# A fused attention, token-mix and channel kernel: divisions and low words moved to GpSimd, new planner costs and tables, own banks for the last products

## The chip, the cores and the metric

The kernel runs on one core of a Trainium2 chip. The metric is the device time of the program in microseconds (us); smaller is better. The engines are named as in the profile: PE (TensorE's matmuls), DVE (VectorE), ACT (ScalarE), POOL (GpSimd) and SP (the queue that issues the transfers).

## What is computed

Four batches of 576 tokens, eight heads of 64. Three layers follow each other:

```python
# 1. attention, window 32; heads 4..7 take every 4th token of a window of 128
scores = scale * q @ k.T, masked;  attn = softmax(scores)
x = attn @ v                                   # (4, 576, 512)
# 2. token mix
xk = mu_k * x + (1 - mu_k) * x_prev            # x_prev: the token before
xr = mu_r * x + (1 - mu_r) * x_prev
v = relu(xk @ w_k) ** 2 @ w_v                  # 512 -> 1024 -> 512
y = sigmoid(xr @ w_r) * v
# 3. low rank over tokens, then a channel MLP, 512 -> 2048 -> 512
u = y + (y.T @ U @ V).T
out = u + relu(u @ w_ch1) @ w_ch2
```

## The kernel before

*Attention* goes by units of a batch, a part of its tokens and a pair of heads. `attend` does one unit (the four of the first part of batch 0), `attend2` two at once. A unit has stages: scores on PE ("qk"), minimum and mask on DVE (`low`, L549), exponentials on ACT (L558), the inverse of the sums on DVE (`inv`, L563 and L564), the division (`norm`, L575, on the engine that the table `NORM_ENG` names for the unit), transposes on PE ("tr", L655 and L741), a copy to SBUF on ACT, the product with v ("pv", L667 and L759), and a copy into the x of the batch. A *visit* is one step of a pair of units: the later half of the old pair (tr, pv) and the scores of the new.

*Token mix.* The 2304 tokens go in 8 chunks of 288. `mix` makes one operand of one pair of heads: the difference `d` = x - x_prev on POOL (L359), then d * mu + x_prev on DVE (L796). For chunk 0 that is multiplied with the whole fp32 weights (`r_row` L855 with four products for each pair, `k_row` L870, then L839). For later chunks operand and weight are split into a high and a low fp32r word and each product is three (high x high, L842; low weight, L843; low operand, L844). The high word is a copy on ACT, the low word a subtraction on the engine that `XK_ENG` names for chunk 1, and on POOL for later chunks. Weights arrive as 64-bit floats in 20 pieces and are converted by `cv_bits`: one ACT step, two DVE steps with a scalar (L398, L399) and two with two tensors (L401, L404).

*Stage 3.* `product` multiplies blocks of 256 by seven products in place of eight (L1076 to L1078), in groups of 256 and four times 512 tokens; `ch1` sums them (L1113) and makes the hidden block as `hh` (ACT) and `hl` (DVE, L1091 and L1133); `ch2` multiplies these with the rows of the second weight into four banks (L1155 to L1157) and, at the last block of a group, adds u and stores (L1175). In the last group the output o = 3 is split at column 384 (`ENDS`), so its ends are stored separately.

*What sets the order.* Every operation is first recorded, with its engine, an estimated duration (`pe`, `dve`, `act`, `sub`, `normed`), what it reads and writes. The code order of the recording comes from the tables at the top: `MIX0` and `MIX` (after which quantum of a chunk which operand of the next is mixed), `VISIT0` and `VISIT` (at which quanta attention takes a step), `LOADS`, `UV_AT`, `PREP`, `SPLIT` (when which weight piece is split). `plan` then runs a list schedule over the estimates, 24 times, with ranks from a pass backwards, from which `EARLIER` takes microseconds for some kinds; DVE and POOL exclude each other in it for operations marked `lock`. The best pass is issued as one order for each engine. Into gaps of PE of more than 0.6 us in the plan it puts matmuls on `zero` (fillers, L1358), whose results are not used. So all engines run fixed orders, and an operation that waits holds up all behind it on its engine.

## Time and profile before

| | us |
|---|---|
| median of 3 runs | 745.29 (744.68 to 746.07) |
| profiled execution, its own time | 745.44 |
| its span, first to last instruction | 743.7 |
| PE busy | 734.8 (99%) |
| DVE busy | 564.2 (76%) |
| ACT busy | 393.9 (53%) |
| POOL busy | 365.2 (49%) |
| chain that ended last | PE 89%, DVE 7%, ACT 2%, issue 1% |

[...] The chain is followed back from the last instruction, at each step to what released it. PE's granted clock was 9 tenths or more in all 40 slices of the span. Times in timelines are from the start of the span, and matmuls overlap, so their pace is the distance of their starts.

### The profile page before, as it was taken

The page shows a single profiled execution, that of the slowest core. Times are in us where ns is not written, and L with a number is a line of the kernel's source. Part 1 is how long each engine was busy: PE and PEld are TensorE (multiplying, and loading weights), DVE is VectorE, ACT ScalarE, POOL GpSimd, SP SyncE. Part 2 cuts the span into 40 slices and gives each one's busy share as a digit, 9 for nine tenths or more (in the row PEclk, how much of TensorE's full clock was granted, in tenths as well). Part 3 has the DMA queues.
Part 4 walks back from the last instruction along what each step waited for, and adds up shares of the span by engine and source line. Part 5 has one row for each costly group of instructions (what it writes and reads, how often), then busy time and mean ns, then how long its engine had stood idle before and what let it go on. Part 6 is the DMA issues. An engine that isn't in the chain of part 4 may idle for free.

```text
span 743.7 us, 18335 instructions
## 1 busy us (share of the span) xinstructions
PE 734.8 (99%) x6936; PEld 678.0 (91%) x6936; DVE 564.2 (76%) x1353; ACT 393.9 (53%) x1003; POOL 365.2 (49%) x380
## 2 busy tenths in 40 slices
PE   8999999999999999999999999999999999999998
PEld 6777999999999999999999989889889988898886
DVE  6999999899998945885679687676988765575532
ACT  5696795858585746473546444444444433343310
POOL 0100274746473635283776477344878544365500
PEclk9999999999999999999999999999999999999999
DMA  8877338658757640557633451134413212141001
GB/s 317 290 260 238 124 114 274 229 198 264 229 167 252 210 129 15 204 174 244 220 104 114 142 185 43 53 133 139 152 43 109 91 43 86 43 138 62 15 1 57
DMA packets 53224, 109.78 MB, mean 148 GB/s; under 512 B 5648, under 2 KB 15888, under 8 KB 53136
## 3 DMA queue, kind: packets, MB, share of 16 engines
q1 hardware_dynamic: 53136, 108.62, 44.0%
q8 instruction: 54, 0.88, 0.5%
q14 instruction: 34, 0.28, 0.1%
HBM read 86.05 MB, written 22.54 MB: 146 GB/s over the span
## 4 chain that ended last, share of the span: by engine, by line
PE 89%; DVE 7%; ACT 2%; issue 1%; DMA 0%; POOL 0%; DVEq 0%
PE psM L842 10%; PE psM L843 10%; PE psM L844 10%; PE psS L1157 9%; PE psS L1155 9%; PE psS L1156 9%; PE psM L1076 8%; PE psM L1078 8%; PE psM L1077 8%; PE psS L759 2%; DVE wx L401 1%; PE psS L703 1%; DVE wx L398 1%; PE psM L839 1%; DVE wx L404 1%
## 5 line engine op out<-in xcount | busy, mean ns | idle before, releaser
L359 POOL TENSOR_TENSOR cl<-sums,ch 128x512 fp32r<-128x512 f32 x72 | 98.3, 1366 | 83.1 <-ACT ch L364 51.5
L364 ACT ACTIVATE ch<-sums 128x512 fp32r<-128x512 f32 (+1 forms) x104 | 57.2, 562 | 118.5 <-DVE sums L484 111.9
L1155 PE MATMUL psS<-hh,rh 128*128 128x512 f32 (+2 forms) x322 | 119.6, 371 | 0.2 <-ACT hh L1132 0.2
L1157 PE MATMUL psS<-hl,rh 128*128 128x512 f32 (+2 forms) x322 | 119.8, 372 | 0.0
L1156 PE MATMUL psS<-hh,rl 128*128 128x512 f32 (+2 forms) x322 | 119.5, 371 | 0.0
L842 PE MATMUL psM<-xk,wh 128*128 128x288 f32 x336 | 101.0, 301 | 0.0
L843 PE MATMUL psM<-xk,wl 128*128 128x288 f32 x336 | 99.1, 295 | 0.0
L844 PE MATMUL psM<-xk,wh 128*128 128x288 f32 x336 | 98.9, 294 | 0.0
L359 POOL TENSOR_TENSOR cl<-st,ch 128x256 fp32r<-128x256 f32 x80 | 65.7, 830 | 49.4 <-PE psM L1078 42.5
L484 DVE TENSOR_TENSOR sums<-st 128x256 f32<-128x256 f32 (+1 forms) x144 | 81.5, 615 | 11.0 <-POOL cl L359 11.0
L1157 PEld LDWEIGHTS psS<-hl,rh 128*128 128x128 f32 x322 | 60.7, 188 | 11.2 <-DVE hl L1133 0.4
L1155 PEld LDWEIGHTS psS<-hh,rh 128*128 128x128 f32 x322 | 60.7, 189 | 10.0 <-ACT hh L1132 0.6
L1156 PEld LDWEIGHTS psS<-hh,rl 128*128 128x128 f32 x322 | 60.7, 188 | 9.6
L359 POOL TENSOR_TENSOR k2s<-k,k2s 128x288 fp32r<-128x288 f32 x49 | 46.4, 950 | 43.3 <-ACT k2s L364 42.1
L842 PE MATMUL psM<-k2s,wh 128*128 128x288 f32 x224 | 67.2, 300 | 0.0
L843 PE MATMUL psM<-k2s,wl 128*128 128x288 f32 x224 | 66.1, 295 | 0.2 <-issue 0.2
L844 PE MATMUL psM<-k2s,wh 128*128 128x288 f32 x224 | 66.0, 294 | 0.0
L842 PEld LDWEIGHTS psM<-xk,wh 128*128 128x128 f32 x336 | 63.0, 188 | 0.6
L843 PEld LDWEIGHTS psM<-xk,wl 128*128 128x128 f32 x336 | 63.1, 188 | 0.1
L844 PEld LDWEIGHTS psM<-xk,wh 128*128 128x128 f32 x336 | 63.2, 188 | 0.0
L1133 DVE SCALAR_TENSOR_TENSOR hl<-ort,hh 128x512 fp32r<-128x512 f32 x32 | 26.3, 820 | 44.8 <-ACT hh L1132 44.8
L359 POOL TENSOR_TENSOR xk<-m,xk 128x288 fp32r<-128x288 f32 x48 | 44.0, 928 | 28.7 <-ACT xk L364 22.1
(157 smaller groups left out, 2130.8 us busy)
## 6 DMA issues: line engine op xcount, KB each, us to landing
st<-w2f SPq DMA_DIRECT2D x96, 256.0 KB, 3.0
w<-w2raw SPq DMA_DIRECT2D x32, 512.0 KB, 4.9
w<-w1raw SPq DMA_DIRECT2D x20, 512.0 KB, 5.2
w2f<-w SPq DMA_DIRECT2D x32, 256.0 KB, 2.6
raw<-qk SPq DMA_DIRECT2D x16, 320.0 KB, 6.2
ytmp<-y SPq DMA_DIRECT2D x32, 144.0 KB, 2.1
yb<-ytmp SPq DMA_DIRECT2D x4, 1152.0 KB, 6.5
uf<-us SPq DMA_DIRECT2D x32, 144.0 KB, 1.9
```

What stands on the lines that cost most here:

```text
L359: op("POOL", t, lambda: nc.gpsimd.tensor_tensor(out=out_(), in0=a(), in1=b(), op=ALU.subtract), r, w, 40, lock=True)
L364: act(n, lambda: nc.scalar.activation(out_(), in_(), AF.Copy), r, w, psum, strided)
L484: dve(k * Q, lambda: nc.vector.tensor_tensor(out=q(sm_, n, k)(), in0=a(), in1=b(), op=op_), [(s1,), (s2,)], [(sm_, key)], two=True)
L842: nc.tensor.matmul(a, lhsT=wh, rhs=xh, start=start, stop=False)
L843: nc.tensor.matmul(a, lhsT=wl, rhs=xh, start=False, stop=False)
L844: nc.tensor.matmul(a, lhsT=wh, rhs=xl, start=False, stop=stop)
L1076: nc.tensor.matmul(a, lhsT=wh()[:, wi], rhs=xh()[:, ci], start=(k == 0), stop=False)
L1077: nc.tensor.matmul(a, lhsT=wl()[:, wi], rhs=xh()[:, ci], start=False, stop=False)
L1078: nc.tensor.matmul(a, lhsT=wh()[:, wi], rhs=xl()[:, ci], start=False, stop=(k == len(parts) - 1))
L1155: nc.tensor.matmul(a, lhsT=wh, rhs=xh, start=(j == 0 and e == 0), stop=False, skip_group_check=c0 > 0)
L1156: nc.tensor.matmul(a, lhsT=wl, rhs=xh, start=False, stop=False, skip_group_check=c0 > 0)
L1157: nc.tensor.matmul(a, lhsT=wh, rhs=xl, start=False, stop=(j == 7 and e == 1), skip_group_check=c0 > 0)
```

## The change

- The divisions of all units go to POOL (`NORM_ENG`): 10 leave DVE (four of 64, four of 320, two of 256 elements) and those of one pair of units leave ACT, where they were 8 instructions more. The low words of chunk 1's operands go to POOL (`XK_ENG`): 8 leave DVE. The differences `d` were there before.
- The planner's costs of small PE products are lowered (scores 28 to 25 ns each, transposes 108 to 101 or 91, pv 34 to 33), loads run at 320 in place of 285 GB/s and begin at 0.7 us (`FIRST`), and `EARLIER` names other kinds.
- The tables `MIX`, `MIX0`, `VISIT0`, `VISIT`, `LOADS`, `UV_AT`, `PREP` and `SPLIT` have other numbers.
- In the last `ch2` of the last group the two ends of o = 3 are summed into banks of their own (`tails`), while what o = 3 holds from the blocks before is added to u ahead of them (`sum3`); each end is then one addition more.

```diff
-MIX = ((4, 0, "r"), (8, 1, "r"), (12, 0, "k"), (13, 2, "r"), (14, 1, "k"), (14, 2, "k"), (18, 3, "r"), (19, 3, "k"))
-MIX0 = ((7, 0, "r"), (8, 1, "r"), (13, 0, "k"), (13, 2, "r"), (14, 1, "k"), (17, 2, "k"), (15, 3, "r"), (19, 3, "k"))
-VISIT0 = (0, 4, 9)
-VISIT = (0, 11)
+MIX = ((6, 0, "r"), (5, 1, "r"), (12, 0, "k"), (13, 2, "r"), (16, 1, "k"), (14, 2, "k"), (18, 3, "r"), (19, 3, "k"))
+MIX0 = ((7, 0, "r"), (7, 1, "r"), (13, 0, "k"), (13, 2, "r"), (14, 1, "k"), (17, 2, "k"), (18, 3, "r"), (19, 3, "k"))
+VISIT0 = (0, 4, 12)
+VISIT = (1, 9)
...
-PREP = (0, 5, 13)
+PREP = (0, 4, 12)
...
-NORM_ENG = ("DVE", "DVE", "ACT", "DVE", "POOL")
+NORM_ENG = ("POOL", "POOL", "POOL", "POOL", "POOL")
 MIX_ENG = ("POOL", "POOL")
-XK_ENG = "DVE"
-EARLIER = {"d": -20, "k2": -10, "wx": -5, "cl": 5}
-RATE = 285.0
+XK_ENG = "POOL"
+EARLIER = {"d": -15, "st": -2, "tr": -2, "tA": -2, "tB": -2}
+RATE = 320.0
+FIRST = 700.0
...
             free = dict.fromkeys(("PE", "DVE", "ACT", "POOL", "SP"), 0.0)
+            free["SP"] = FIRST
...
-        pe(3 * 108, tr, [(pr,), ("cst",)], [(pt,)], "tr")
+        pe(3 * 101, tr, [(pr,), ("cst",)], [(pt,)], "tr")
...
-        pe(nw * 4 * 28, qk, [(rq, x * QKW) for x in range(2)], [(x,) for x in sc], "qk")
+        pe(nw * 4 * 25, qk, [(rq, x * QKW) for x in range(2)], [(x,) for x in sc], "qk")
...
-        end = g == len(GROUPS) - 1 and j == 7
+        last = g == len(GROUPS) - 1
+        end = last and j == 7
+        if end:
+            tails = {c0: bank("M") for c0, _ in ENDS}
+            sum3 = Lazy([P, n], F32, "d", "ot", 2)
+            dve(n, lambda: nc.vector.tensor_tensor(
+                out=sum3(), in0=accs[g][3](), in1=ug[g]()[:, 3, :], op=ALU.add),
+                [(accs[g][3],), (ug[g],)], [(sum3, c0) for c0, _ in ENDS], two=True, psum=True)
...
+            apart, shut = end and o == 3, 6 if last and o == 3 else 7
+            if apart:
+                acc = tails[c0]
...
+                if last and o == 3:
+                    t = tails[c0]
+                    from_, plus, keys = (lambda t=t, c=c: t()[:, : c.stop - c.start]), (lambda ot=ot, c=c: ot()[:, c]), [(t,), (ot, c0)]
```

What this does to the orders stands here at three places. In these rows a line is the instruction, what it writes and reads, its size and how many follow each other; `zero` is a filler, `raw` attention's q, k and v, `pr` its scores, `pts` their transposes, `xk` a mix of chunk 0, `wx` a whole weight. Lines from the middle of the file on are two higher in the changed kernel, those at the fillers 16.

PE's order near the start, from the transposes of the third unit on, before:

```order
L655 MATMUL psS<-cst_t,pr 128x128 x3
L1358 MATMUL psS<-zero 128x512 x2
L667 MATMUL psS<-pts,raw 64x32 x20
L1358 MATMUL psM<-zero 128x224 x6
L855 MATMUL psM<-xk_307,wx 128x288 x4
L1358 MATMUL psS<-zero 128x512 x2
...
L703 MATMUL psS<-raw 32x64 x32
L855 MATMUL psM<-xk_307,wx 128x288 x4
L1358 MATMUL psM<-zero 128x224 x7
L855 MATMUL psM<-xk_307,wx 128x288 x4
```

And in the changed kernel:

```order
L1374 MATMUL psS<-zero 128x512 x16
L657 MATMUL psS<-cst_t,pr 128x128 x3
L1374 MATMUL psS<-zero 128x512 x2
L669 MATMUL psS<-pts,raw 64x32 x20
L657 MATMUL psS<-cst_t,pr 128x128 x3
L1374 MATMUL psS<-zero 128x512 x3
L669 MATMUL psS<-pts,raw 64x32 x20
L705 MATMUL psS<-raw 32x64 x32
L1374 MATMUL psM<-zero 128x224 x16
L857 MATMUL psM<-xk_307,wx 128x288 x12
```

The products of `r_row` for the pairs 1, 2 and 3, which stood in three places between the stages of attention, now stand in a row behind all of them, and no filler comes after them.

DVE's order ahead of the mix of pair 1, before:

```order
L399 TENSOR_SCALAR wx<-wx 128x512
L404 SCALAR_TENSOR_TENSOR wx<-w_148,wx 128x512
L401 SCALAR_TENSOR_TENSOR wx<-w_150,wx 128x512
L796 SCALAR_TENSOR_TENSOR xk_307<-d,mu_t,x_95 128x288
L404 SCALAR_TENSOR_TENSOR wx<-w_150,wx 128x512
```

And in the changed kernel:

```order
L400 TENSOR_SCALAR wx<-wx 128x512 x2
L401 TENSOR_SCALAR wx<-wx 128x512 x2
L403 SCALAR_TENSOR_TENSOR wx<-w_402,wx 128x512
L403 SCALAR_TENSOR_TENSOR wx<-w_414,wx 128x512
L406 SCALAR_TENSOR_TENSOR wx<-w_402,wx 128x512
L406 SCALAR_TENSOR_TENSOR wx<-w_414,wx 128x512
...
L551 ISA pr,mn<-psS,cst_t 128x64
L551 ISA mn 128x1
L798 SCALAR_TENSOR_TENSOR xk_307<-d,mu_t,x_95 128x288 x2
```

The mix (L796, now L798) has moved behind more conversions and four score steps, and the mix of pair 2 follows it at once. Counted from the mix of pair 0, there are 13 steps with a scalar and 14 with two tensors in between, where 5 and 5 were; no division, where two stood; two pairs for the inverse, where one stood; ten score steps, where six stood. On POOL three `d` and the divisions of two units stand up to there, where one `d` stood.

PE's order at the last block of the first group of stage 3 (`hh` and `hl` with their numbers; each block has six rows for each bank), before:

```order
L1155 MATMUL psS_5587<-hh_5935,rh_5889 128x256
L1156 MATMUL psS_5587<-hh_5935,rl_5917 128x256
L1157 MATMUL psS_5587<-hl_5943,rh_5889 128x256
L1076 MATMUL psM_6047<-tA_5556,ch_6024 128x256
...
L1155 MATMUL psS_5568<-hh_6039,rh_5979 128x256
L1156 MATMUL psS_5568<-hh_6039,rl_6006 128x256
```

And in the changed kernel:

```order
L1168 MATMUL psS_5574<-hh_5937,rh_5877 128x256
L1169 MATMUL psS_5574<-hh_5937,rl_5925 128x256
L1170 MATMUL psS_5574<-hl_5945,rh_5877 128x256
L1168 MATMUL psS_5553<-hh_6024,rh_5968 128x256
L1169 MATMUL psS_5553<-hh_6024,rl_6010 128x256
L1170 MATMUL psS_5553<-hl_6030,rh_5968 128x256
```

The products of the next group that stood between the last two blocks (some 40 rows) have moved behind the first six rows of the last. In both orders the products that make the last hidden block stand just ahead of the six rows of the block before it.

At the very end DVE's order was three additions of 512, then those of 384 and 128 columns; now it is the partial sum of o = 3 and one addition of 512, then 384 and 128 (the ends, each from its own bank), then two additions of 512. PE's last product is 512 columns wide, where it was 128.

## Rows read from the trace of the kernel before

**Rows 1.** Windows: us, busy us and instructions of PE, PEld, DVE, ACT, POOL; clock, DMA.

```profile
77.00:130.00 53.00, 53.00 (x783) 52.06 (x782) 51.02 (x153) 39.98 (x120) 25.62 (x30) 1.00 0.53 173
...
290.00:740.00 450.00, 449.63 (x2978) 413.52 (x2976) 311.63 (x562) 192.13 (x388) 244.34 (x230) 1.00 0.32 106
```

**Rows 2.** Groups by line: the wide fillers; busy us, mean ns.

```profile
L1358 PE MATMUL psS<-zero 128*128 128x512 f32 x39 | 14.1, 491 | 1.5 <-DVE zero L1354 1.5
```

**Rows 3.** Timeline of PE, 15 to 78 us: start, duration, instruction, count, idle before.

```profile
24.03 2.21 PE L855 MATMUL psM<-xk,wx 128*128 128x288 f32 x8 [0.86 <-DVE xk L796]
...
38.71 1.14 PE L759 MATMUL psS<-pts,raw 64*64 64x32 f32 x64
...
40.56 6.57 PE L870 MATMUL psM<-xk,wx 128*128 128x288 f32 x26
...
48.13 7.92 PE L839 MATMUL psM<-xk,wx 128*128 128x288 f32 x32
55.88 0.60 PE L741 MATMUL psS<-cst_t,pr 128*128 128x128 f32 x4
...
76.83 0.51 PE L842 MATMUL psM<-xk,wh 128*128 128x288 f32 x1
```

**Rows 4.** Timeline of DVE and POOL, 14 to 25 and 64 to 71 us.

```profile
15.18 0.51 DVE L796 SCALAR_TENSOR_TENSOR xk<-d,mu_t,x 128x288 f32<-128x288 f32 x1
...
18.18 0.74 DVE L575 TENSOR_TENSOR pr<-pr,sm 128x64 f32<-128x64 f32 x2
...
19.80 0.71 POOL L359 TENSOR_TENSOR d<-x 128x288 f32<-128x288 f32 x1 [6.04 <-ACT x L364]
...
19.91 0.89 DVE L398 TENSOR_SCALAR wx<-wx 128x512 f32<-128x512 f32 x1
20.83 0.22 DVE L549 CUSTOM_DVE_ANT_0 pr<-psS,cst_t 128x64 f32<-128x64 f32 x1
...
23.46 0.51 DVE L796 SCALAR_TENSOR_TENSOR xk<-d,mu_t,x 128x288 f32<-128x288 f32 x1
...
67.02 0.42 DVE L398 TENSOR_SCALAR wx<-wx 128x512 f32<-128x512 f32 x1
...
68.03 1.29 DVE L401 SCALAR_TENSOR_TENSOR wx<-w,wx 128x512 int32<-128x512 int32 x2
69.23 1.29 DVE L404 SCALAR_TENSOR_TENSOR wx<-w,wx 128x512 int32<-128x512 int32 x2
```

**Rows 5.** Groups by line and form: the low word of a mix on both engines.

```profile
L361 DVE TENSOR_TENSOR xk<-m,xk 128x288 fp32r<-128x288 f32 x8 | 3.5, 449 | 0.0
...
L359 POOL TENSOR_TENSOR xk<-m,xk 128x288 fp32r<-128x288 f32 x48 | 44.0, 928 | 28.7 <-ACT xk L364 22.1 <-PE psM L844 6.0
```

**Rows 6.** Timeline of PE, ACT and DVE, 382 to 393 us.

```profile
385.66 0.28 PE L1155 MATMUL psS<-hh,rh 128*128 128x256 f32 x1
...
386.25 0.28 PE L1157 MATMUL psS<-hl,rh 128*128 128x256 f32 x1
...
391.84 0.28 PE L1155 MATMUL psS<-hh,rh 128*128 128x256 f32 x1
...
385.92 0.60 ACT L1090 ACTIVATE hh<-psM 128x512 fp32r<-128x512 f32 x1 [3.23 <-PE psM L1078]
...
383.31 2.93 DVE L361 TENSOR_TENSOR rl<-st,rh 128x512 fp32r<-128x512 f32 x2
386.55 0.69 DVE L1091 SCALAR_TENSOR_TENSOR hl<-psM,hh 128x512 fp32r<-128x512 f32 x1 [0.31 <-ACT hh L1090]
```

**Rows 7.** Timeline of DVE, 736 to 744 us, and DMA issues of the end (us to landing).

```profile
738.35 0.69 DVE L1175 TENSOR_TENSOR ot<-psS,ug 128x512 f32<-128x512 f32 x1 [3.51 <-PE psS L1157]
740.00 0.76 DVE L1175 TENSOR_TENSOR ot<-psS,ug 128x384 f32<-128x384 f32 x2 [0.97 <-PE psS L1157]
...
out<-ot SPq DMA_DIRECT2D x3, 256.0 KB, 2.0
...
out<-ot SPq DMA_DIRECT2D x1, 64.0 KB, 1.6
```

## The prediction

> **What bounds the kernel now.** The median of the three runs is 745.29 us; the profiled execution took 745.44, with a span of 743.7, and every sum below is made against that execution, which stands 0.15 us above the median. I read four views. The windows [rows 1] show the reader that from 290 to 740 us TensorE was busy 449.63 of 450 us, and from 77 to 130 us all 53.00; DVE had 2 us to spare in that second stretch and far more in the first. So once the split products have begun, only a new stall can lengthen the run. The groups by line [rows 2] show matmuls on `zero`, which are the planner's fillers: the 39 wide ones alone are 14.1 us that are only there because TensorE had nothing to do. The timeline of TensorE [rows 3] shows that they sit before 76.83 us, when the first split product (L842) starts. That start is the first thing the change can shift. The timeline of DVE and GpSimd [rows 4] tells what sets it: DVE, with conversions of weights, scores, divisions and mixes in one queue. The second thing is a stall in the middle, the third the end.

> **The change, part by part.**

> *The start.* The four products of `r_row(1)` wait for the mix of pair 1. Before, that mix started at 23.46, 8.28 us after that of pair 0 (15.18) [rows 4], and the products started at 24.03 [rows 3]. In the new order DVE has much more between the two mixes: 13 two-scalar steps of a conversion where 5 stood, 14 two-tensor steps where 5 stood, a second pair for the inverse and four more score steps; the two divisions are gone. Three steps took .335 each from 67.02 to 68.03, and two took .60 each from 68.03 to 69.23 [rows 4]. That gives 8 x .335 = 2.7 and 9 x .60 = 5.4; the score steps are bounded by 4 x .22 = .9 [rows 4], which I take whole because it has to pay for the inverse too; the pair of divisions that left DVE gives back .74 [rows 4]. GpSimd now has two divisions and two `d` more in that stretch. The row for that: `d` ran .71 from 19.80, and the conversion step that started at 19.91 took .89 where the same step took .42 at 67.02, so it cost DVE .47 [rows 4]. Two `d` at .47, and a division of 64 + 320 elements at .63 each (more than one `d`, less than its length), are 2.2. The sum is 2.7 + 5.4 + .9 - .7 + 2.2 = 10.5, so the mix starts near 34.0 and the products at 34.5, 10.5 us later than before.

> What TensorE must still do from there is unchanged work: 76 whole-weight products (12 of r, 32 of k, 32 of v). The 32 records that began at 48.13 are 16 products and lasted until 55.88, so one takes .484 [rows 3], and 76 take 36.8. Between them lie three visits, 1.85 each (38.71 to 40.56 [rows 3]; the third has five windows for four, 2.3), so 6.0, and their transposes, .60, .60 and .75, from the row at 55.88 [rows 3]: 8.0 together. Three small waits remain in the new order (a mix behind conversions, a second half of transposes behind GpSimd's second division, k's second mix); the wait of this kind before was .86 [rows 3], so they lie between 0 and 2.6, and I take 1.8, since the queues are fuller. The split products would start at 34.5 + 36.8 + 8.0 + 1.8 = 81.1. But the new order has done one visit more by then, 2.3 + .6 = 2.9 of work, so no change would be 79.7. **Term: +1.4.** From below it is bounded by what leaves DVE (the first rival, -2.0); from above by +3.0, where the four locks (two `d`, two divisions) cost GpSimd's whole lengths and the waits their 2.6.

> The 10 divisions, 8 low words and 8 of ScalarE's small divisions that move are otherwise hidden under TensorE, which is full; without that cover a low word costs .928 on GpSimd against .449 on DVE [rows 5].

> That price of a lock stands on a row. [...]

> *The middle.* When the first group of the second stage ends, the last rows of `ch2` need `hh` and `hl` of the last hidden block. Before, some 40 rows of the next group's products stood between the previous block's six rows and these: the six began at 385.66, the next six of `ch2` at 391.84 [rows 6]. Now the first of these follow at once. ScalarE finished `hh` at 385.92 + .60 = 386.52 and DVE `hl` at 386.55 + .69 = 387.24 [rows 6]. The six rows start .118 apart (385.66 to 386.25), so TensorE would be ready at 386.37 and ask for `hl` two rows later, at 386.6: it waits to 387.3, **+.7** at least. If DVE comes there later, by the 1.6 us by which two locked low words at 383.31 (2.93) exceed two free ones at .69 [rows 6], it waits 2.3. DVE had been only .31 idle ahead of `hl`, so I take **+1.2**, nearer the lower end. In other places too an operand now ends just ahead of its product (a visit in chunk 1 behind a division on GpSimd, low words of W2): 0 to two instructions of .69, and as TensorE lost almost nothing there before [rows 1], I take **+.5**.

> *The end.* Before, the two last additions took .76 from 740.00, and 64 KB landed 1.6 us after issue. Now the partial sum and the two ends of o = 3 come earlier, and a whole block of 512 is last: its addition takes .69, its 256 KB 2.0 [rows 7]. That is -.07 + .4, and the last matmul ends a little earlier: **+.25**, between 0 and .4. So the separate banks do not hold the last products.

> Sum: 1.4 + 1.2 + .5 + .25 = 3.35, thus 748.8 for a profiled execution, **748.6** on the median. About 0.2% (1.5 us) is what can be told from no change: faster is below 743.8, slower above 746.8.

> **The rivals.** *Relief wins (the other side).* Before 70 us DVE sheds four pairs of divisions at .74 [rows 4] and three low words at .449 [rows 5], 4.3 us, and pays five more locks at .47 (2.4). If the twentieth conversion, and not the mix of pair 1, sets the start, the split products begin 2.0 earlier for the same work; it decides if the products of pair 1 start before 34.5 - 1.4 - 2.0 = 31.1. With no new stall and the end at +.25: 743.5 on the median, and less if the locks fall beside scores. For it: the conversions end late, at 69.23 + 2 x .60 = 70.4 [rows 4], and the split products start only 6.4 behind. Against it: the products now stand in a row behind that mix.

> *It cancels.* Relief and longer queue balance, and only the .7 wait and the end remain: 746.2.

> *The lock takes over.* From 77 to 130 us DVE had 53 - 51.0 = 2.0 to spare [rows 1]. Each low word or division moved frees .45 but can block DVE for .93 [rows 5]; eight of them are 3.8, and 1.8 goes beyond the spare time, to TensorE, on top of my sum: 750.4. For it: the operations are late in the planner's queue; against it: DVE's PSUM reads need no lock. [...]

> *The banks do nothing.* If the separate banks do let the ends go early and DVE would have been ready anyway, only the .25 is off; it moves no sign.

> **How the numbers follow.** Forecast .53 (about .49 slower, .04 same); relief .17 (.15 faster, .02 same); cancelling .18 (.14 same, .04 slower); lock .12, slower. That makes faster .15, same .20, slower .65. The range reaches from the relief, 743.5, to the forecast with the upper bound for the start and half of it for the wait, 748.6 + 1.6 + .55 = 750.75, rounded to 751 (the forecast's own range is 746.5 to 751). It leaves out the cases below the relief and those where all upper bounds meet.

> **What would show it.** Right: fewer fillers; `r_row(1)` between 33 and 36, its three products in a row; the first split product near 81; a wait of TensorE on DVE's `hl` at about 390 us; a 256 KB transfer last. Wrong: `r_row(1)` before 31 or a split start before 79; no wait at `hl`; or waits of TensorE between 80 and 130 us that end on DVE or GpSimd.

## The result, and the profile of the changed kernel

The changed kernel takes **756.44 us** in the median of five runs (754.53 to 758.00), the kernel before 745.41 in the runs beside it: a ratio of 1.0148, with a 95% interval of 1.0137 to 1.0160. It is slower, as forecast, but by 11.0 us where 3.3 were forecast, and 756.4 lies outside the range of 743.5 to 751.0. The profiled execution took 757.69, with a span of 755.9; the one before took 745.44. So 12.25 us have to be found in the trace.

The page gives the first reading (busy time by engine; then the chain that ended last):

```profile
PE 739.2 (98%) x6932; PEld 679.0 (90%) x6932; DVE 559.5 (74%) x1336; ACT 393.0 (52%) x995; POOL 386.9 (51%) x400
...
PE 78%; DVE 8%; DMA 6%; ACT 4%; issue 2%; POOL 1%; SPq 0%; DVEq 0%; ACTq 0%
```

TensorE is 4.4 us busier and still a smaller part of the chain, and 2% of the chain is "issue": time in which an engine waited for nothing that the profile shows. GpSimd has 21.7 us more. The two windows that answer to [rows 1]:

```profile
77.00:130.00 53.00, 53.00 (x772) 51.35 (x771) 47.29 (x142) 38.34 (x116) 27.10 (x30) 1.00 0.44 141
290.00:740.00 450.00, 446.83 (x2974) 410.40 (x2973) 308.48 (x560) 195.55 (x397) 250.37 (x234) 1.00 0.32 105
```

From 77 to 130 us nothing was lost, and DVE had become freer there (47.29 where 51.02 stood). From 290 to 740 us TensorE lost 3.2 us where it had lost .4. The waits of TensorE from 80 to 752 us say on what (line, releaser, us in total, times, longest):

```profile
PE psS L705 <- issue: 2.8, 2, 1.7
PE psS L1170 <- DVE hl L1093: 0.8, 1, 0.8
PE psS L1169 <- DVE rl L363: 0.6, 1, 0.6
PE psS L969 <- ACT yh L366: 0.5, 1, 0.5
PE psS L761 <- ACT pts L366: 0.5, 1, 0.5
PE psM L969 <- DVE yl L363: 0.3, 1, 0.3
PE psS L969 <- DVE yl L363: 0.2, 1, 0.2
PE psS L1168 <- ACT hh L1134: 0.2, 1, 0.2
```

The greatest entry is not a wait for an operand. TensorE stood still twice in the middle of a visit's scores. The timeline at the first of these (start, duration, instruction, count, idle before):

```profile
153.53 1.37 PE L761 MATMUL psS<-pts,raw 64*64 64x32 f32 x80
154.83 1.02 PE L705 MATMUL psS<-raw 64*32 64x64 f32 x78
157.52 0.30 PE L705 MATMUL psS<-raw 64*32 64x64 f32 x2 [1.67 <-issue]
157.75 0.45 PE L844 MATMUL psM<-k2s,wh 128*128 128x288 f32 x1
157.99 0.44 PE L845 MATMUL psM<-k2s,wl 128*128 128x288 f32 x1
```

Of 80 products 78 were issued, and the last two came 1.9 us later, although by the profile's names they read and write what the 78 did. Behind the stop the split products start .24 apart, where they start .13 apart elsewhere. The windows there show why (second number: TensorE's busy time; third from the end: the granted clock):

```profile
155.00:157.00 2.00, 0.85 (x78) 0.69 (x64) 2.00 (x6) 0.70 (x2) 1.49 (x2) 1.00 0.23 74
157.00:159.00 2.00, 1.48 (x8) 1.39 (x9) 1.68 (x22) 1.91 (x5) 0.38 (x1) 0.74 0.58 182
159.00:161.00 2.00, 2.00 (x10) 2.00 (x10) 0.30 (x3) 2.00 (x14) 0.00 (x0) 0.50 0.95 334
161.00:163.00 2.00, 2.00 (x16) 2.00 (x15) 1.50 (x4) 1.37 (x7) 0.00 (x0) 0.91 0.94 359
```

The granted clock fell from 1.00 to .50 at 157.96 us and was 1.00 again from 161.37 on, 3.4 us later: 15 products .11 longer each, 1.6 us, on top of the stop. A row with its count shows the second stop:

```profile
213.71 0.30 PE L705 MATMUL psS<-raw 64*32 64x64 f32 x4 [1.12 <-issue]
```

**The account**, by the distances of TensorE's starts beyond their usual pace (these run a little longer than the idle in brackets, which counts from a matmul's modelled end):

| part | us |
|---|---|
| first split product at 82.33, before 76.83; 2.86 of work done ahead | +2.64 |
| stops without a releaser: 1.88 and 1.33, against one of .37 before | +2.84 |
| lower clock behind the first | +1.6 |
| waits for operands: near 210 (.64), 332 (1.49), 373 (.81), 396 (1.61), 416 (.71) | +5.26 |
| end | 0 |
| sum | 12.3 |

The 2.86 are a visit (80.02 to 82.33) and its transposes (75.50 to 76.05) that the new order does ahead of the split products. TensorE at the start:

```profile
25.45 0.55 PE L657 MATMUL psS<-cst_t,pr 128*128 128x128 f32 x3 [1.48 <-POOL pr L577]
...
28.85 0.55 PE L657 MATMUL psS<-cst_t,pr 128*128 128x128 f32 x3 [0.86 <-POOL pr L577]
...
32.11 2.05 PE L1374 MATMUL psM<-zero 128*128 128x224 f32 x16
34.15 4.15 PE L857 MATMUL psM<-xk,wx 128*128 128x288 f32 x16
38.73 2.21 PE L857 MATMUL psM<-xk,wx 128*128 128x288 f32 x8 [0.44 <-DVE xk L798]
41.64 1.24 PE L872 MATMUL psM<-xk,wx 128*128 128x288 f32 x4 [0.70 <-ACT sg L366]
...
56.54 4.15 PE L841 MATMUL psM<-xk,wx 128*128 128x288 f32 x16 [0.24 <-ACT rt L901]
...
63.62 1.14 PE L761 MATMUL psS<-pts,raw 64*64 64x32 f32 x64 [0.55 <-ACT pts L366]
...
82.33 0.40 PE L844 MATMUL psM<-xk,wh 128*128 128x288 f32 x1
```

### The profile page after: what moved, and what is told of

The parts are those of the page before. It is cut to its first block, busy times and chain, and to the rows that moved or that the text cites. A ratio compares the mean times of both kernels' runs of the same rounds, so it can differ in the third digit from the quotient of the medians.

```text
span 755.9 us, 18331 instructions
## 1 busy us (share of the span) xinstructions
PE 739.2 (98%) x6932; PEld 679.0 (90%) x6932; DVE 559.5 (74%) x1336; ACT 393.0 (52%) x995; POOL 386.9 (51%) x400
## 4 chain that ended last, share of the span: by engine, by line
PE 78%; DVE 8%; DMA 6%; ACT 4%; issue 2%; POOL 1%; SPq 0%; DVEq 0%; ACTq 0%
PE psM L844 9%; PE psM L846 8%; PE psM L845 8%; PE psS L1170 8%; PE psS L1169 8%; PE psS L1168 8%; PE psM L1078 7%; PE psM L1080 7%; PE psM L1079 7%; PE psS L761 2%; PE psM L841 2%; DMA w<-w1raw 2%; DMA ug<-uf 2%; PE psS L705 1%; ACT pr L560 1%
## 5 line engine op out<-in xcount | busy, mean ns | idle before, releaser
L1170 PE MATMUL psS<-hl,rh 128*128 128x512 f32 (+1 forms) x318 | 118.6, 373 | 0.8 <-DVE hl L1093 0.8
L1169 PE MATMUL psS<-hh,rl 128*128 128x512 f32 (+1 forms) x318 | 118.4, 372 | 0.7 <-DVE rl L363 0.6
L1168 PE MATMUL psS<-hh,rh 128*128 128x512 f32 (+1 forms) x318 | 118.4, 372 | 0.2 <-ACT hh L1134 0.2
L361 POOL TENSOR_TENSOR cl<-st,ch 128x256 fp32r<-128x256 f32 x80 | 67.9, 861 | 47.7 <-PE psM L1080 39.8
L486 DVE TENSOR_TENSOR sums<-st 128x256 f32<-128x256 f32 (+1 forms) x144 | 79.7, 603 | 11.9 <-POOL ch L361 7.6
L361 POOL TENSOR_TENSOR xk<-m,xk 128x288 fp32r<-128x288 f32 x56 | 54.5, 988 | 37.8 <-ACT xk L366 30.4
L361 POOL TENSOR_TENSOR k2s<-k,k2s 128x288 fp32r<-128x288 f32 x49 | 44.6, 912 | 39.4 <-ACT k2s L366 38.2
L577 POOL TENSOR_TENSOR pr<-pr,sm 128x320 f32<-128x320 f32 (+2 forms) x36 | 26.6, 738 | 64.3 <-DVE sm L566 37.6
```

The costliest lines, as they stand in the source:

```text
L361: op("POOL", t, lambda: nc.gpsimd.tensor_tensor(out=out_(), in0=a(), in1=b(), op=ALU.subtract), r, w, 40, lock=True)
L486: dve(k * Q, lambda: nc.vector.tensor_tensor(out=q(sm_, n, k)(), in0=a(), in1=b(), op=op_), [(s1,), (s2,)], [(sm_, key)], two=True)
L1168: nc.tensor.matmul(a, lhsT=wh, rhs=xh, start=((j == 0 or apart) and e == 0), stop=False)
L1169: nc.tensor.matmul(a, lhsT=wl, rhs=xh, start=False, stop=False)
L1170: nc.tensor.matmul(a, lhsT=wh, rhs=xl, start=False, stop=((j == shut or apart) and e == 1))
```

## The experiments

Each part of the change was first put into the kernel before by itself; then the count of TensorE's instructions was varied. "Split start" is the start of the first split product, with a star where the visit of 2.86 us is done ahead of it; "stops" are TensorE's stops without a releaser after 70 us, by distances of starts.

| kernel | median | ratio, 95% | split start | stops |
|---|---|---|---|---|
| before | 745.41 | | 76.83 | .37 |
| changed | 756.44 | 1.0137 to 1.0160 | 82.33* | 1.88, 1.33 |
| e1 engines alone | 749.53 | 1.0039 to 1.0069 | 80.98* | 1.93, .40 |
| e2 planner's costs alone | 753.07 | 1.0076 to 1.0116 | 79.87 | .89 |
| e3 tables alone | 755.62 | 1.0113 to 1.0163 | 77.77 | 3.23, 1.85, 2.68, 2.26 |
| e4 banks alone | 745.25 | .9993 to 1.0012 | 76.37 | .21 |
| e5 changed, fillers halved | 756.01 | 1.0103 to 1.0165 | 83.25* | 1.76, 1.35 |
| e6 tables, fillers halved | 750.30 | 1.0039 to 1.0071 | 79.93 | 1.15 |
| e7 before, fewer fillers | 748.47 | 1.0026 to 1.0063 | 77.79 | 1.60, 1.19, .56 |
| e8 `EARLIER` alone | 746.82 | 1.0008 to 1.0027 | 76.54 | .48 |
| e9 changed, fillers in thirds | 761.76 | 1.0188 to 1.0235 | 87.55* | .34 |
| e10 products' costs alone | 748.24 | 1.0029 to 1.0065 | 84.59* | 1.95 |
| e11 loads' costs alone | 751.91 | 1.0076 to 1.0103 | 80.60* | .32, .61, 1.33 |
| e12 before, fillers in thirds | 754.11 | 1.0097 to 1.0128 | 84.70 | .97 |
| e13 changed, small fillers | 758.83 | 1.0177 to 1.0221 | 87.07* | none |
| e14 before, small fillers | 749.31 | 1.0042 to 1.0068 | 80.41 | .60 |
| e15 changed, loads' costs of before | 751.68 | 1.0063 to 1.0097 | 78.69 | 1.71, 1.16, 1.53 |

### The parts alone

**e1**, the engines of the divisions and low words:

```diff
-NORM_ENG = ("DVE", "DVE", "ACT", "DVE", "POOL")
+NORM_ENG = ("POOL", "POOL", "POOL", "POOL", "POOL")
-XK_ENG = "DVE"
+XK_ENG = "POOL"
```

> The kernel before with one edit alone: divisions and low words on GpSimd, old tables, old costs, old banks. The port theory (what is lost comes from operations on GpSimd that block DVE) expects most of the 11 us here: 752 to 757 us, and waits of TensorE on DVE or GpSimd between 77 and 130 us. The order theory (the loss comes from the new tables and costs) expects 745.4 within 1.5 us, up to 2.5 us faster if DVE's relief counts.

It took 749.53, between the two forecasts. TensorE did not wait for GpSimd or DVE between 77 and 130 us, so the rival of the lock has nothing to stand on. Its greatest waits after 70 us:

```profile
PE psM L842 <- issue: 2.0, 2, 1.7
PE psS L967 <- DVE yl L361: 0.7, 2, 0.4
```

The split start is 80.98, with 2.86 of work done ahead: +1.3. The waits at L967 stand where the changed kernel has those of 332 us, and the rest is stops on issue.

**e2**, the planner's costs alone (`RATE`, `FIRST`, `EARLIER`, and the four estimates of small products):

```diff
-EARLIER = {"d": -20, "k2": -10, "wx": -5, "cl": 5}
-RATE = 285.0
+EARLIER = {"d": -15, "st": -2, "tr": -2, "tA": -2, "tB": -2}
+RATE = 320.0
+FIRST = 700.0
...
-        pe(nw * 4 * 28, qk, [(rq, x * QKW) for x in range(2)], [(x,) for x in sc], "qk")
+        pe(nw * 4 * 25, qk, [(rq, x * QKW) for x in range(2)], [(x,) for x in sc], "qk")
```

> The kernel before with the planner's costs alone (small products, loads, first load, EARLIER). The order theory expects a loss here or in the next run, the two together about 11 us: taken evenly 748 to 753 us. The port theory expects 745.4 within 1.5 us. If the wait that ends on DVE's hl at the last block of the first group of stage 3 (1.1 us in the changed kernel) comes from the costs, it stands here too.

753.07, at the upper end of what the order theory gave. The waits in the first group of stage 3 are those of the changed kernel (.65 and .82 by the view there):

```profile
368.83 0.39 PE L1158 MATMUL psS<-hh,rl 128*128 128x256 f32 x1 [0.55 <-DVE rl L363]
...
392.97 0.39 PE L1159 MATMUL psS<-hl,rh 128*128 128x256 f32 x1 [0.81 <-DVE hl L1093]
```

So the wait at `hl` that was forecast is real, and the planner's costs make it. They also put the split start 3.0 later.

**e3**, the tables alone (`MIX`, `MIX0`, `VISIT0`, `VISIT`, `LOADS`, `UV_AT`, `PREP`, `SPLIT` as changed, all else as before):

```diff
-MIX = ((4, 0, "r"), (8, 1, "r"), ...
+MIX = ((6, 0, "r"), (5, 1, "r"), ...
-VISIT = (0, 11)
+VISIT = (1, 9)
```

> The kernel before with the tables alone (MIX, MIX0, VISIT0, VISIT, LOADS, UV_AT, PREP, SPLIT). The order theory expects the larger part of the late start here (2.6 us in the changed kernel, after the work that was moved ahead is taken off): 747 to 753 us, with the products of r_row(1) late. The port theory expects 745.4 within 1.5 us.

755.62, above the forecast and nearly all of the loss of the whole change. The late start that was expected here came to .9 us only (77.77 in the table), and the waits are hardly on operands. Waits of TensorE, the greatest three, and two rows of its timeline:

```profile
PE psS L703 <- issue: 3.7, 2, 2.1
PE psM L843 <- issue: 3.1, 1, 3.1
PE psM L844 <- issue: 2.5, 1, 2.5
```

```profile
141.93 0.29 PE L843 MATMUL psM<-xk,wl 128*128 128x288 f32 x1 [3.06 <-issue]
...
215.49 0.30 PE L844 MATMUL psM<-xk,wh 128*128 128x288 f32 x1 [2.51 <-issue]
```

Four stops, 10.0 us in all: here the loss is not where an operand comes late.

**e4**, the banks alone (the two ends of o = 3 in `tails`, as in the diff of the change):

> The kernel before with the banks of the last products alone. All theories expect 745.4 to 745.8 us: the end is within 0.3 us in both profiles (3.73 us from TensorE's last product to the end of the span before, 3.72 after). If the banks do shorten the end where the two ends are last, 744.8.

745.25, no change that can be told.

**e8**, `EARLIER` alone:

```diff
-EARLIER = {"d": -20, "k2": -10, "wx": -5, "cl": 5}
+EARLIER = {"d": -15, "st": -2, "tr": -2, "tA": -2, "tB": -2}
```

> The kernel before with the table EARLIER alone. If the waits on low words and hidden blocks in the first group of stage 3 (0.7, 1.6, 0.2 and 0.5 us with all the costs) come from EARLIER, they stand here, without any more work on GpSimd: 748 to 749.5 us. If they come from the costs of products and loads, or from GpSimd, 745.3 within 1 us.

746.82, between the two forecasts and 1.3 us above the kernel before, and no wait at `rl` or `hl` before 560 us. **e10** and **e11** split the rest of e2. e10 has the products' costs (scores 28 to 25, pv 34 to 33, transposes 108 to 101 or 91):

```diff
-        pe(nw * 4 * 28, qk, [(rq, x * QKW) for x in range(2)], [(x,) for x in sc], "qk")
+        pe(nw * 4 * 25, qk, [(rq, x * QKW) for x in range(2)], [(x,) for x in sc], "qk")
```

> The kernel before with the lowered planner costs of TensorE's small products alone (scores 25, transposes 101 and 91, pv 33); loads and EARLIER as before. If these costs make the waits of the last block of the first group of stage 3: TensorE waits .6 to .8 for rl and 1 to 1.6 in all for hh and hl between 365 and 400 us, +2. If they come from the loads' costs: no wait there. Besides, by the instruction count one visit is at risk, the one with five windows near 155 us (edge at 316 of its 320): a stop of about 1.9 and up to 1.6 of lower clock. So 745.4 + 2 + 1.9 to 3.5 = 749 to 751 with the middle waits, 747 to 749 without; the start can add up to 2 in either.

748.24 (747.13 to 752.0; the profiled execution is the slowest). No wait in stage 3 beyond the .2 for `hh` that the kernel before has too, but a stop of 1.95 in the visit that the count had named. e11 has the loads' costs:

```diff
-RATE = 285.0
+RATE = 320.0
+FIRST = 700.0
```

> The kernel before with the planner's costs of the loads alone (320 GB/s and a first load at 0.7 us); products' costs and EARLIER as before. If these make the waits of the last block of the first group: .6 to .8 for rl and 1 to 1.6 for hh and hl between 365 and 400 us, +2. If they come from the products' costs: none there. By the instruction count three visits after 70 us are at risk (edges at 286 of 288, 294 of 288 and 316 of 320, near 103, 140 and 153 us): stops of 0 to 3.2 each. 748 to 752 with the middle waits, 746 to 750 without.

751.91, with the wait for `rl` (at 368.5 us, 1.5 where e2 has .55), none of note for `hl`, and stops in the three visits that the count had named:

```profile
PE psS L1158 <- DVE rl L363: 1.5, 1, 1.5
PE psS L705 <- issue: 1.1, 1, 1.1
PE psM L845 <- issue: 0.4, 1, 0.4
```

So the loads' costs alone make the wait for `rl`; that for `hl` none of the three costs makes alone. **e15** is the other direction: the changed kernel with the loads' costs of before.

```diff
-RATE = 320.0
-FIRST = 700.0
+RATE = 285.0
+FIRST = 0.0
```

> The changed kernel with the load costs of before (285 GB/s, first load at 0); all else as changed. If these costs make the waits in stage 3's first group: the waits for rl near 373 and for hl near 396 us (.65 and 1.61 in all) are gone, -2.3. If the products' costs, the engines or EARLIER make them: still there. The number of instructions ahead changes, and by the count four visits are at risk of a stop (near 85, 140, 213 and 230 us), 0 to 3 each, so the time can be 753 to 759 in either case; the waits decide.

751.68, below the forecast and 4.8 less than the changed kernel. All of its waits after 70 us:

```profile
PE psS L705 <- issue: 3.8, 3, 1.5
PE psS L1168 <- ACT hh L1134: 0.2, 1, 0.2
```

All five operand waits of the account are gone, that at 332 us too, and three stops stand in their place. What the loads' costs do is seen on DVE, which in the changed kernel stands 7.0 us for transfers between 353 and 364 us:

```profile
DVE us L991 <- DMA uf<-us: 3.6, 2, 1.9
DVE tmp L1060 <- DMA ug<-uf: 3.4, 1, 3.4
```

The second of these waits is 3.2 to 4.3 us in the six profiled kernels that are planned at 320 GB/s and .7 to 2.5 in the eleven others, and in just those six TensorE waits for `rl` between 355 and 385 us. In the changed kernel DVE idles from 363.65 us on for only 1.5 us until 373.10, when it starts that `rl`, straight behind other work. So at 320 GB/s loads stand earlier in the plan than they land, and as DVE's order is fixed, what waits for a transfer makes all behind it late. The link from this wait to the late `rl` is read from the order of the queue; no run moved these transfers alone. ScalarE's waits for pieces of the second weight (2.5 us in all) end at 377.75 and 380.02 us, too late to make it. The wait for `hl` is one of the order: in e15 other products stand again between the six rows of the last two blocks (none of `ch2` starts between 388.03 and 390.86), in the changed kernel none do.

### The count of TensorE's instructions

A stop that no operand explains, in the densest bursts of small products, led to the instructions themselves. The page of the changed kernel has a queue of instructions whose size fits them (queue, kind: packets, MB, share):

```profile
q8 instruction: 54, 0.88, 0.5%
```

0.88 MB in 54 is 16 KB each, and 6932 matmuls and 6932 weight loads over 54 are 257. So a transfer seems to bring 256 of TensorE's instructions, a matmul being two with its load; the 158 products of the visit ahead of the stop are 316. An edge is here the place where one such block of 256 ends and the next begins; most edges cost no stop (28 stops at 806 edges, see below). One such transfer was issued at 154.75 us, when TensorE was some 160 instructions into the visit, and landed at 156.10; TensorE resumed at 157.52. The other was issued at 211.45, landed at 212.37, and TensorE resumed at 213.71. A view of the first stretch, 154 to 157 us:

```profile
q8 instruction: 1, 0.02, 2.8%
```

The theory, the author's estimate from these times: the block behind an edge is asked for at about the time when TensorE passes the edge before it. With the edges placed as below, the transfers of the changed kernel were issued .2 to 4.6 us ahead of that edge from 290 us on, and .78 and .75 us behind it in the two visits that stopped. Among split products 256 instructions last some 17 us (128 products of .13). In a visit they last under 2 us (316 from 153.53 to 155.85), no longer than the transfer with what follows it (1.35 and 1.42 us at 154.75). A visit of four or five windows in which one edge falls soon after its start thus meets the next edge near its end before the block is there.

**e5** halves the first 32 of the wide fillers, all before the visits: same columns, 64 instructions (matmuls and loads) more ahead of everything.

```diff
+                halves = 2 if wide == CW and split < HALVED else 1
+                split += halves > 1
+                for h in range(halves):
+                    n = wide // halves
...
```

> The changed kernel, in which 32 of the 48 wide fillers are issued as two halves: the same columns, 32 matmuls and 64 instructions of TensorE more ahead of the split products, nothing else moved. The instruction theory (TensorE's instructions come in transfers of 16 KB; where the edge of one falls into a dense visit, TensorE runs out of them and stands still, without any operand being late) expects the stops of 1.9 us at 156 and 1.3 us at 212 us and the slow clock behind the first of them to go: 751 to 752.5 us. The operand theory (those stops are waits for data that the profile cannot name) expects 756.4 within 1.5 us, with the stops in place.

756.01, above what the instruction theory gave and in the range of the operand theory, which had the stops in their places. They were not: the stop at 212 us went, that of 156 became 1.35 at 159.8, and a new one of 1.76 came at 102. The count moves the stops, as the theory says; which edges would stop TensorE the forecast did not foresee well enough. **e6** does the same to the tables of e3, with 40 fillers halved:

> The kernel before with the tables of the change (755.6 us) and 40 wide fillers issued as two halves, 80 instructions of TensorE more. The instruction theory expects all four stops (3.2, 1.9, 2.7 and 2.3 us) to go: 745 to 748 us. The operand theory, and the theory that the tables' order itself is slow, expect 755.6 within 2 us.

750.30, above the 745 to 748 of the forecast: all four stops of e3 gone, but one of 1.15 at 86 us new and the split start 2.2 later. That is 5.3 us less than e3 with 80 instructions more.

**e7** takes instructions away: in the kernel before, `FILL` goes from 0.7 to 0.5, which leaves 20 fillers out.

> The kernel before with the planner's share of filled gaps at 0.5 in place of 0.7: 20 fillers, 40 instructions of TensorE, less, no other order. The instruction theory expects edges of transfers near the start of four later visits (40 to 48 instructions in), and so stops of 1 to 3 us without a releaser in two to four of them: 748 to 755 us. The operand theory expects 745.3 within 1 us, since the fillers do nothing.

748.47. Products whose results nobody uses were taken out, and the kernel became .4% slower: three stops, where the count had given two to four.

**e9** and **e12** split wide fillers into three (44 in the changed kernel, 23 in the one before), to set the count where no visit is at risk:

```diff
+                parts = (176, 168, 168) if wide == CW and split < SPLIT3 else (wide,)
+                split += len(parts) > 1
+                c = CW - wide
+                for n in parts:
...
```

> The changed kernel, with 44 of its wide fillers issued as three matmuls of 176, 168 and 168 columns: the same columns, 88 products (176 instructions with their loads) more, all ahead of 80 us. Instruction-supply theory: every later product moves by 176 places against the edges of the transfers; by the offsets read from the traces so far the second edge of no visit after 70 us then falls into its last third or just behind it, so TensorE has no stop that ends on issue after 70 us, and the clock does not fall: 757.7 - 4.8 = 752.9 for the profiled execution, 751 to 753.5 for the median (the start may move by one). The waits on operands (209, 331, 373, 396, 416 us) stay. Rival, the stops belong to the order of the operations and not to the number of instructions ahead of them: stops near 156 and 212 us as in the changed kernel, 755.5 to 758.

> The kernel before, with 23 of its wide fillers issued as three matmuls of 176, 168 and 168 columns: 46 products (92 instructions) more, all ahead of 77 us. Instruction-supply theory: the one stop of the kernel before that ends on issue (.37 at 152.7 us) goes and none comes, so 745.4 - .4 = 745.0, 744.3 to 745.8. Rival, more instructions cost time by themselves or make new stops: 746 or more.

Both times failed: 761.76 and 754.11. The stops went as expected (only .34 is left in e9; in e12 that of 152 us went and one of .97 came at 257), but the fillers became long. Groups by line, e12, where [rows 2] had 14.1 us for 39:

```profile
L1364 PE MATMUL psS<-zero 128*128 128x168 f32 (+2 forms) x85 | 21.7, 428 | 1.4 <-DVE zero L1355 1.4
```

Thirds start .22 apart near 5 us (27 in 6.0 us), nine wide ones there .41: three thirds are .66 for the columns of one. So the split start moved by 7.9, and by 5.2 in e9. The runs could not say what the stops cost. **e13** and **e14** therefore put in small products in attention's shape, which were taken to start .018 apart (by the distances of the starts it is .017 in the later units and .032 in the first four):

```diff
+                for s in range(small):
+                    nc.tensor.matmul(onto()[:64, :32], lhsT=zero[:64, :64], rhs=zero[:64, :32], start=True, stop=True)
```

> The changed kernel, with 8 of the 16 wide fillers that stand before 24 us replaced by 94 small ones (weights 64 x 64, 32 columns, the shape of attention's products, which start .018 apart in the trace): 8 x .246 = 1.97 us of fillers go, 94 x .018 = 1.7 come, and 86 products (172 instructions) more stand ahead of all that follows. [...] Instruction-supply theory: no stop on issue near 156 and 212 us, granted clock 1.0 there, split start 81.5 to 83; 757.7 - 4.8 = 752.9 for the profiled execution, median 751 to 754, the waits on operands at 331, 373, 396 and 416 us still there. Rival, the stops belong to the order and not to the count: 755.5 to 758 with stops near 156 and 212.

> The kernel before, with 4 wide fillers near 35 us replaced by 48 small ones (weights 64 x 64, 32 columns): 44 products (88 instructions) more at no time of their own (4 x .29 go, 48 x .018 come). Instruction-supply theory: the stop of .37 near 152 us goes; a visit whose block edge falls some 30 places behind its end, near 250 us, may stop for up to 1. So 744.5 to 746, split start 76 to 77. [...]

Again the times failed, 758.83 and 749.31, and again at the start. The row of e14, with the products behind it, which took 1.72 in the kernel before:

```profile
35.20 2.97 PE L1363 MATMUL psS<-zero 64*64 64x32 f32 x48
...
38.93 3.09 PE L871 MATMUL psM<-xk,wx 128*128 128x288 f32 x6
```

Onto one and the same region they start .062 apart, and the products behind them are slow; in e13 the granted clock was .81 in the mean from 20 to 30 us and .51 from 30 to 33. But e13 has what was asked for, the changed kernel without stops. Its waits after 70 us, all of them:

```profile
PE psS L1170 <- DVE rl L364: 1.6, 1, 1.6
PE psS L762 <- ACT pts L367: 1.5, 2, 1.2
PE psS L1171 <- DVE hl L1094: 0.8, 1, 0.8
PE psM L970 <- DVE yl L364: 0.3, 1, 0.3
PE psS L1169 <- ACT hh L1135: 0.2, 1, 0.2
```

From the split start to the end its profiled execution (758.38) took 671.3 us, that of the changed kernel 675.4. It is 4.1 shorter there, although its operand waits are 1.0 longer (6.24 against 5.26): stops and lower clock cost the changed kernel about 5, as in the account (1.88 + 1.33 + 1.6 = 4.8). In e14 the stop of 152 us went too; one of .60 at 252 us and a wait of 1.1 for GpSimd at 184 us came.

Over the 17 profiled kernels there are 136 visits of four or five windows between 70 and 300 us. With TensorE's matmuls and loads counted and the edges set every 256, 32 of these have an edge 30 to 76 places behind their start: 24 stopped, for 30 us together. Of 78 with the edge at 77 to 251 places, none did; of the other 26, four.

The traces show more. With TensorE's few other records counted too (semaphores and drains, 125 in the changed kernel), all 28 stops of the table fall at one and the same place of the 256. Such places are the edges: with transfers and edges paired in order, TensorE passed 806 of them after 70 us in the 17 traces, none sooner than 1.2 us after its block had landed, and at the 28 stops it resumed 1.2 to 1.6 us after the landing. So the visits that stopped had reached an edge before that time; the visits with an edge near their start that did not stop reached theirs later.

## Why the direction was right and the size wrong

- **The step that failed** is the sentence that, once the split products have begun, only a new stall can lengthen the run, together with the list of what could stall: an operand, the lock, the end. The sum had no term for TensorE's own instructions and none for its clock. By the account these were 2.8 of stops and 1.6 of lower clock. The kernel before showed it already, in a small "issue" wait at L843 behind 152.7 us (.37 by the starts), which was not read; its waits of TensorE from 70 to 740 us have the line

```profile
PE psM L843 <- issue: 0.2, 1, 0.2
```

- **The middle** was right in place, mechanism and nearly in size: forecast +1.2 at `hl`, 1.61 measured with what `hh` and `rl` add in the same six rows (.20, .32, 1.09). The reason held too: two low words of 2.38 together stand ahead of `hl` on DVE, which starts at 397.23, and ScalarE's `hh` had been ready by 396.27 (395.67 + .60):

```profile
394.92 2.38 DVE L363 TENSOR_TENSOR rl<-st,rh 128x512 fp32r<-128x512 f32 x2
397.23 0.68 DVE L1093 SCALAR_TENSOR_TENSOR hl<-psM,hh 128x512 fp32r<-128x512 f32 x1
```

- **Other places**, +.5 with an upper end of 1.4, measured 3.65 (.64, 1.49, .81, .71). A late `rl` in an earlier block, `yh` and `yl` and the `pts` of a visit were not looked for. e15 shows that these too go when the loads' costs do, a part of the change that the prediction had not costed at all; e1 shows that the engines alone also make part of the waits at 332 us. That is 3.2 above the term, the second great miss of the sum.
- **The start** was +2.64 against +1.4, within the bounds of -2.0 to +3.0. The queue on DVE was well estimated in sum: the mix of pair 1 started at 33.58, forecast 34.0, and `r_row(1)` at 34.15, forecast 34.5. In part that is luck: TensorE came to `r_row(1)` straight from its fillers (32.11), without a wait, after waits of 1.48 and .86 for GpSimd's divisions. The stretch behind it was short: 46.6 were forecast, 48.2 measured, and the split start stood at 82.33 in place of 81.1. Four waits stand in it, .44 for the mix of pair 3, .70 for ScalarE's `sg`, .24 for `rt` and .55 for `pts`; by the distances of the starts they are 2.8, where 1.8 was allowed. The rest is spread over the visits and the steps from one kind of product to the next. The upper bound took a lock at GpSimd's whole length; in the kernel before, a conversion step of .42 took .88 to .89 beside a `d` of .71, .96 and 1.12, so some .47 more each time. Fewer fillers were forecast, and there were 64 where 68 stood, though 48 wide ones where 44 stood.
- **The end**, +.25, was 0: from the last product to the end of the span 3.73 us before and 3.72 after. A 256 KB transfer was the last, as said.
- **Rivals.** Relief and cancelling fell with the split start. The lock taking over from 77 to 130 us fell: TensorE lost nothing there, and DVE gained 3.7 us of spare time. What was said against it has numbers in the trace of the kernel before: DVE's mask steps of 64 columns, which read PSUM (L549), took .22 with GpSimd busy all through them (79 steps) as with it idle (37), while sums of 256 columns in SBUF (L484) took .42 with it idle (70) and 1.08 in the mean with it busy all through (13). That the banks do nothing is shown by e4.

What e1, e2 and e3 lose by themselves (4.0, 7.2 and 10.3 by their ratios) is 21.5 together, twice the whole change's 11.0. The parts do not add: each sets the order and the instruction count, and so the start, the waits and the stops, anew. A share of the 11.0 for each part is therefore not to be had; the account by mechanism is. No version tried beats the kernel before by more than the noise.

## What to carry to other kernels

Where an engine runs small instructions in dense bursts, read its waits on "issue" and the row of the instruction queue, and count where the edges of the blocks fall (here every 256): edits ahead of the burst, even of fillers alone, moved the stops (64 instructions more in e5, 40 fewer in e7). Test the parts of a change alone and compare the waits, not only the times, since two variants can be equally slow for different reasons. A planner's cost that is a little too hopeful (here the loads' rate) can come out far from the loads themselves, where a fixed order lets what waits for data hold up all behind it.
